# An attention and gated feed-forward kernel on one core: the first eight heads' key and value summaries handled by matrix products instead of copies, and a new order of the opening

## The chip, the core and the metric

The kernel runs on one core of a Trainium2 chip. Five engines work side by side, each through its own list of instructions in order: PE (TensorE, matrix products), DVE (VectorE), ACT (ScalarE), POOL (GpSimd) and SP (which here issues the loads). A wait in one engine's list holds everything behind it in that list. The metric is the time of one execution on the device, in microseconds (us).

## What is computed

`q`, `k`, `v` have 4 batches, 8 heads, 768 positions and 64 features. Attention looks at a band of neighbours and at one summary for each block of 32 keys:

```
k_sum = max of k over each block of 32 ; v_sum = mean of v over each block of 32
scores_l = scale * q @ k.T, kept where |pos_q - pos_k| < 16, else -1e9
scores_s = scale * q @ k_sum.T + log(32)
a = softmax(concat(scores_l, scores_s)) ; x = a @ concat(v, v_sum)
```

The heads are laid side by side (512 features), then a gated layer follows: `h = max(x @ w_in, 0)` (1024 wide), a convolution of three taps over positions, `gate = sigmoid(conv)`, and `(h * gate) @ w_out`. All is in fp32; a product with weights is made of three products of rounded parts (high by high, high by low, low by high).

## The kernel before

**Tiles and stages.** A batch's 768 positions are two chunks of 384. A chunk has four pairs of heads; pair `n` counts through all chunks (`n = 4 * chunk + pair`, so chunk 0 is `n = 0..3`, chunk 1 is `n = 4..7`). For a pair the kernel loads queries, keys and values, makes the key summaries `ks` (a maximum on DVE) and the value summaries `vs` (a sum on DVE, turned by a product `pv` on PE and scaled to means `vm` on ACT), multiplies queries with 96 near keys and 24 summaries for each block of 64 queries (`qk`, 120 columns), masks (`masked`, DVE), exponentiates (`expo`, ACT), normalises (`norm`, POOL or DVE), turns the weights (`turn` on PE, `turned` copies them out) and multiplies with the values (`av`). The result is split in a high and a low part (`xh`, `xl`), goes through `f1` (eight groups `fc` of 128 hidden features, four parts `cc` of three products each), the gates (`R` relu, `T` middle tap, `D` the two other taps on DVE, `H` tanh on ACT, `G` product on DVE, `C` and `O` high and low part) and `f2` (tokens `p` in the opening).

**Two regimes.** Chunks 0 and 1, all decoding of the weights, the attention of chunk 2 and some of chunk 3's are an opening whose order is written out by hand: the string `ORDER` is a list of tokens, each of which is one step with its pair or group number and, after a slash, the engine that does it (`n2.1/v`: normalise head 1 of pair 2 on DVE). Every engine's own list follows the tokens. `Z` tokens are products on zeros that only keep PE busy (`zeros`, L112). From chunk 2 on a loop (`unit`, `slot`, `slot_av`) sets the order; it starts with the turn of pair 12's second head and `f1` of chunk 2. A scheduler orders the loop's instructions on DVE, POOL and SP, and may place them ahead of the last tokens; on PE it follows the code.

**The weights** come as 64-bit words. A weight tile `i` of 16 (8 of `w_in`, 8 of `w_out`) is loaded (`w` or `W`, 512 KB), its words decoded on ACT (`wy`) and DVE (`wl`, `wu`) and split into a high part (`wh`, ACT or POOL) and a low part (`wo`, POOL). The tiles of `w_out` go through the tag `stage`, two buffers, which the value tiles `vt` of later chunks share.

**Chunk 0.** Each pair's keys are loaded once whole (`load_k`), and `key_rows` (tokens `kc`, L146) copies the overlapping near keys from there into `kw`, beside which `key_sums` (tokens `kb`, L271, POOL) repeats the summaries for all six blocks. The value means are repeated in `va` by `val_wide` (tokens `vc`, L295, POOL). Later chunks load near keys and near values ready cut (`load_kw`, `load_v`) and repeat the means by a DMA (`load_vm`).

Of the kernel before, what the change touches and what calls it, by code (L numbers as in the profile page):

```python
# [51 lines left out]
c3.0/s xl2 tr3.1 a6 wy1 wl1 f0.0.0 c3.1/s wu1 av3 wh1/s k10 wl2 wy2 f0.0.1 wo1 xh3/v xl3 w6
f0.0.2 wy3 wu2 f0.1.0 M4 wl3 f0.0.3 wh2/s wu3 f0.1.1 wo2 R0.0/v wh3/s w7 f0.1.2 T0.0/s wy4
wl4 f0.2.0 wo3 D0.0 f0.1.3 a7 wy5 f0.2.1 wu4 R0.1/s q4 H0.0 f0.2.2 wl5 T0.1/s G0.0 wh4/s
f0.2.3 wu5 M5 f0.3.0 C0.0/g D0.1 wh5/s M6 wo4 R0.2/s f0.3.1 T0.2/v H0.1 f0.3.2 q5 wo5 G0.1
D0.2 f0.4.0 C0.1/g f0.3.3 q6 wy6 wl6 f0.4.1 q7 H0.2 wu6 R0.3/s f0.4.2 G0.2 wh6/s f0.5.0 K5
wl7 C0.2/s wo6 wy7 f0.4.3 K6 wy8 f0.5.1 M7 R0.4/s qk4 wu7 wy9 O0.0 f0.5.2 wh7/s q8 K7 wl8
T0.3/s f0.5.3 m4.0 O0.2 W10 e4.0 wu8 m4.1 O0.1 R0.5/s e4.1 wl9 kb5 D0.3 t8 wh8/g T0.4/s
T0.5/s kb6 ks9 wo8 H0.3 ks10 k11 wo7 Z11 p0.0 r4 D0.5 qk5 kb7 n4.1/g q9 D0.4 wy10 K8 n4.0/g
H0.5 G0.3 vs8 tr4.0 H0.4 m5.0 f0.6.0 c4.0/s m5.1 tr4.1 e5.0 f0.6.1 c4.1/s wu9 pv8 e5.1  # L60
f0.6.2 C0.3/g G0.5 wl10 vm8 f0.6.3 kb8 ks11 wh9/s t9 O0.3 av4 t10 C0.5/s r5 R0.6/s wu10 qk6
a8 T0.6/s G0.4 O0.5 xh4/s q10 wh10/s m6.0 f0.7.0 K9 n5.0/g m6.1 e6.0 f0.7.1 xl4 wo10 tr5.0
hx4 e6.1 f0.7.2 vs9 n5.1/g f1.0.0 c5.0/s vs10 t11 f0.7.3 wo9 M8 r6 tr5.1 W11 pv9 D0.6 R0.7/s
# [22 lines left out]
def attention_ffn(ctx, tc, qT, kT, vT, v4, w_in, cwT, w_out, mask8, ident_in, out):  # L86
# [119 lines left out]
    def kw_tile(n):  # L206
        if n == NP - 1:
            kw = sp.tile([P, 1024], F32, tag="stage", name=f"kw{n}", bufs=2)
            of(n)["kw"] = kw[:, : CB * NK].rearrange("p (b k) -> p b k", b=CB)
        else:  # L210
            of(n)["kw"] = sp.tile([P, CB, NK], F32, tag="kw", name=f"kw{n}", bufs=3)
# [608 lines left out]
```

## Time and profile before

| | us |
|---|---|
| median of three runs (lowest, highest) | 401.23 (400.06, 401.51) |
| the profiled execution | 400.0 |
| its span, first to last instruction | 398.2 |

| engine | busy us | share of the span |
|---|---|---|
| PE | 369.2 | 93% |
| DVE | 263.5 | 66% |
| ACT | 236.0 | 59% |
| POOL | 151.6 | 38% |

The span has two parts: up to some 124 us several engines and the loads share the work of the opening, and from there to 394.6 us PE has products without a gap. A mean over both says little; the rows below are taken from each part by itself. A row's "idle before" is the time in which an engine waited ahead of such instructions, and the arrow names what ended the wait.

### The profile page before, as it was taken

The numbers are of one execution on the slowest core, as the hardware profiler recorded it, in microseconds if no ns is written. First come the engines' busy times: TensorE is split into PE (matmuls) and PEld (weight loads), VectorE is DVE, ScalarE is ACT, GpSimd is POOL, SyncE is SP. The second block draws the span as 40 slices with busy tenths as digits, with TensorE's granted clock in tenths as the row PEclk, the third lists the DMA queues.
The fourth block names the chain that finished last, engine by engine and source line by source line (L and its number), as shares of the span: only waits on it lengthen the run. The fifth ranks groups of instructions, "written<-read, shape, count | busy, mean of one in ns | idle before, by whom it ended". The sixth has DMA issues, their size and how long they took to land.

```text
span 398.2 us, 8746 instructions
## 1 busy us (share of the span) xinstructions
PE 369.2 (93%) x3118; PEld 313.2 (79%) x3121; DVE 263.5 (66%) x810; ACT 236.0 (59%) x746; POOL 151.6 (38%) x189
## 2 busy tenths in 40 slices
PE   5768878898996999999999999999999999999996
PEld 2346646687785888888888888988888888999884
DVE  3789899899996465768666556566675755556200
ACT  1765778887564777766565767666656643343211
POOL 2455696776342333333333333333332332222200
PEclk9989999999998999999999999999999999999999
DMA  8999979996755244556332324434310000000011
GB/s 299 316 354 290 239 218 261 286 287 163 251 168 154 81 138 131 159 171 192 77 102 72 97 80 113 114 95 116 93 39 28 28 1 29 26 26 28 26 54 53
DMA packets 45355, 54.29 MB, mean 136 GB/s; under 512 B 24640, under 2 KB 33024, under 8 KB 45312
## 3 DMA queue, kind: packets, MB, share of 16 engines
q1 hardware_dynamic: 41568, 47.19, 41.2%
q10 hardware_dynamic: 3744, 6.54, 4.4%
q8 instruction: 25, 0.41, 0.4%
q14 instruction: 18, 0.15, 0.1%
HBM read 45.36 MB, written 6.29 MB: 130 GB/s over the span
## 4 chain that ended last, share of the span: by engine, by line
PE 70%; DVE 20%; ACT 4%; DMA 3%; issue 2%; SPq 0%; DVEq 0%; ACTq 0%
PE f L615 30%; PE f L512 26%; PE pq L317 5%; PE xp L410 4%; PE pt L394 4%; DVE t L553 4%; DVE a L341 3%; DVE wu L136 2%; ACT a L354 2%; DVE vs L277 2%; DVE wl L130 2%; DVE ks L262 2%; DMA q<-qT 2%; DMA wo<-w_out 1%; DVE a L378 1%
## 5 line engine op out<-in xcount | busy, mean ns | idle before, releaser
L592 POOL TENSOR_TENSOR glo<-t,ghi 128x383 fp32r<-128x383 f32 (+1 forms) x64 | 66.3, 1037 | 125.4 <-ACT ghi L144 110.5
L512 PE MATMUL f<-xh,win_hi 128*128 128x384 f32 (+1 forms) x256 | 91.5, 357 | 4.0 <-DVE t L574 3.5
L553 DVE SCALAR_TENSOR_TENSOR t<-f,cw,t 128x382 f32<-128x382 f32 (+3 forms) x128 | 78.7, 616 | 18.9 <-ACT t L540 15.8
L512 PE MATMUL f<-xh,win_lo 128*128 128x384 f32 (+1 forms) x256 | 87.0, 340 | 1.1 <-POOL win_lo L179 1.1
L512 PE MATMUL f<-xl,win_hi 128*128 128x384 f32 (+1 forms) x256 | 86.7, 339 | 0.0
L354 ACT ACTIVATE a<-a,nm 128x120 f32<-128x120 f32 x192 | 68.7, 399 | 13.3 <-DVE nm L341 12.0
L615 PE MATMUL f<-wout_lo,ghi 128*128 128x512 f32 x192 | 75.4, 393 | 1.0 <-POOL wout_lo L179 1.0
L615 PE MATMUL f<-wout_hi,ghi 128*128 128x512 f32 x192 | 76.0, 396 | 0.3 <-POOL wout_hi L146 0.3
L615 PE MATMUL f<-wout_hi,glo 128*128 128x512 f32 x192 | 74.9, 391 | 0.0
L569 ACT ACTIVATE t<-t 128x383 f32<-128x383 f32 (+1 forms) x64 | 33.7, 527 | 50.0 <-DVE t L553 49.4
L378 POOL TENSOR_TENSOR a<-a,sm 128x360 f32<-128x360 f32 x54 | 42.4, 802 | 48.6 <-DVE sm L373 45.5
L574 DVE SCALAR_TENSOR_TENSOR t<-t,f 128x383 f32<-128x383 f32 (+1 forms) x64 | 35.3, 553 | 31.7 <-ACT t L569 31.7
L512 PEld LDWEIGHTS f<-xh,win_hi 128*128 128x128 f32 x256 | 48.7, 190 | 9.0 <-DVE t L574 5.3
L512 PEld LDWEIGHTS f<-xh,win_lo 128*128 128x128 f32 x256 | 48.4, 189 | 1.7 <-POOL win_lo L179 1.7
L512 PEld LDWEIGHTS f<-xl,win_hi 128*128 128x128 f32 x256 | 48.7, 190 | 1.2
L341 DVE CUSTOM_DVE_ANT_0 a<-pq,mask 128x120 f32<-128x120 f32 x192 | 41.8, 277 | 3.2 <-PE pq L317 2.9
L615 PEld LDWEIGHTS f<-wout_hi,glo 128*128 128x128 f32 x192 | 36.1, 188 | 7.9
L615 PEld LDWEIGHTS f<-wout_hi,ghi 128*128 128x128 f32 x192 | 36.1, 188 | 6.9 <-POOL wout_hi L146 0.8
L394 PE MATMUL pt<-ident,a 128*120 128x128 f32 x192 | 33.4, 283 | 8.6 <-DVE aT L146 3.3
L615 PEld LDWEIGHTS f<-wout_lo,ghi 128*128 128x128 f32 x192 | 36.1, 188 | 6.5 <-POOL wout_lo L179 1.3
L144 ACT COPY aT<-pt 120x384 f32<-120x384 f32 x57 | 28.2, 495 | 18.4 <-PE pt L394 17.8
L530 ACT ACTIVATE f<-f 128x384 f32<-128x384 f32 (+1 forms) x58 | 28.6, 492 | 15.7 <-PE f L512 15.7
(62 smaller groups left out, 465.3 us busy)
## 6 DMA issues: line engine op xcount, KB each, us to landing
va<-v SPq DMA_DIRECT2D x32, 288.0 KB
kw<-kT SPq DMA_DIRECT2D x28, 288.0 KB
q<-qT SPq DMA_DIRECT2D x32, 192.0 KB
out_dram<-ob ACTq DMA_DIRECT2D x24, 256.0 KB
kT<-kT SPq DMA_DIRECT2D x12, 392.0 KB
vt<-vT SPq DMA_DIRECT2D x12, 384.0 KB
wo<-w_out SPq DMA_DIRECT2D x8, 512.0 KB
raw_a<-w_in SPq DMA_DIRECT2D x6, 512.0 KB
```

The lines of the kernel that those rows point to most:

```text
L144: nc.scalar.copy(out, x)
L341: nc.vector.tensor_tensor_reduce(st["a", h][:, i, :], st["pq"][h][:, i * NK : (i + 1) * NK], mask[:, edge(n, i), :], -0.125, 3.0e38, ALU.a ...
L354: this = nc.scalar.activation(st["a", h][:, i, :], st["a", h][:, i, :], AF.Exp, bias=st["nm"][:, h, i : i + 1], scale=-1.0, accum_out=st[" ...
L378: by[eng].tensor_tensor(a, a, s, ALU.mult)
L394: nc.tensor.transpose(pt[:NK, i * P : (i + 1) * P], a[:, i, :], ident)
L512: nc.tensor.matmul(ph[:, :n], w[:, fc, cc, :], x[:, cc, :n], start=(cc == 0 and m == 0), stop=(cc == NCC - 1 and m == 2),)
L530: nc.scalar.activation(h[:, :n], h[:, :n], AF.Relu)
L553: nc.vector.scalar_tensor_tensor(t[:, i0:i1], h[:, hf + k - 1 + i0 : hf + k - 1 + i1], cw[:, fc, k : k + 1], t[:, i0:i1], ALU.mult, ALU.add,)
L569: nc.scalar.activation(t, t, AF.Tanh, scale=0.5)
L574: nc.vector.scalar_tensor_tensor(t, t, 1.0, h[:, hf : hf + ng], ALU.add, ALU.mult)
L592: nc.gpsimd.tensor_tensor(gate_at("lo", c, fc), t, hi.bitcast(F32), ALU.subtract)
L615: nc.tensor.matmul(po, gx[:, fc, ss], w[:, fc, :], start=(fc == 0 and m == 0), stop=(fc == NFC - 1 and m == 2),)
```

## The change

Chunk 0 (pairs 0 to 3) works without the copies. `qk` multiplies with the loaded keys themselves (96 columns), and a new step `q_sums` (token `qs`) multiplies with the summaries (24 columns) for both blocks of 128 queries at once, three blocks and two heads, six products. `val_turn` makes the value sums by six products of the values, loaded with positions on the partitions (`v0`), with a matrix of ones and zeros that stands beside the identity in `consts`; so the four `vs` sums on DVE go. `av` gets one product for each head on the means and twelve on the 96 near values, added up in place. Tokens `kc`, `vc` and four of the `kb` go. `ORDER` is new throughout: the number of tokens of a kind changes only for chunk 0's steps, for the zero products (23 to 43 outside the ten ahead of the list), and for the engine after the slash. From the diff, cut:

```
-k2 k0 t1 k1 q0 k3 q1 ks2 t2 t3 ks0 kc0/g q2 kb0 q3 t0 ks1 kc1/g z qk0 kc2/v kb1 kb2 m0.0 K4
...
-xl10 p1.7 r12 R1.7/s av11 n12.0/v T1.7/s n12.1/g ob1 D1.7 qk13 xh11/s od1 tr12.0 m13.0 H1.7
-xl11 e13.0 G1.7 m13.1 C1.7/g e13.1 c12.0/v O1.7 r13 n13.0/v n13.1/v
+t3 k2 w0 z k0 q0 q1 q2 q3 ks2 pv3 k1 vm3 t2 wy0 wl0 w1 wu0 w2 ks0 K4 Z9 qk0 wh0/v dcw t0 qs0
...
+e11.0 wl14 f1.2.2 D1.1 pv11 tr10.0 e11.1 f1.3.2 wu14 f1.2.3 M12 vm11 c10.0/s r11 f1.3.3 M11
+wh14/s n11.0/v tr10.1 H1.1 n11.1/g R1.2/v qk12 R1.3/s T1.2/s wl15 av9 K15 wo14 G1.1 T1.3/s
...
+e13.0 G1.4 f1.5.3 xl11 e13.1 C1.4/g f1.7.0 R1.5/v p0.1 O1.4 T1.5/v f1.7.1 r13 p0.2 D1.5
+n13.1/g f1.7.2 p0.3 n13.0/v H1.5 f1.7.3 G1.5 C1.5/v p0.4 R1.7/v O1.5 p0.5 p0.6 p0.7 ob0
+f1.6.1 od0 f1.6.2 f1.6.3 R1.6/s T1.6/s T1.7/s D1.6 D1.7 H1.6 G1.6 H1.7 C1.6/v G1.7 O1.6
+C1.7/g O1.7
...
     def val_turn(n):
         pv = ps.tile([P, 512], F32, tag=tag, name=f"pv{n}", bufs=bufs)
-        nc.tensor.transpose(pv[:NB, :P], of(n)["vs"], ident)
+        if n < NP:
+            step = NB // NT
+            for j in range(NT):
+                at = P + NB - step * (j + 1)
+                nc.tensor.matmul(
+                    pv[:NK, :P],
+                    consts[:, at : at + NK],
+                    of(n)["vt"][:, j * P : (j + 1) * P],
+                    start=j == 0,
+                    stop=j == NT - 1,
+                )
+        else:
+            nc.tensor.transpose(pv[:NB, :P], of(n)["vs"], ident)
...
+                if n < NP:
+                    keys = st["k"][r, blk * QB : blk * QB + WK]
+                else:
+                    keys = st["kw"][r, blk, :]
...
+    def q_sums(n):
+        st = of(n)
+        for i in range(CB // 2):
+            for h in range(2):
+                r = slice(h * QB, (h + 1) * QB)
+                nc.tensor.matmul(
+                    st["pq"][h][:, i * NK + WK : (i + 1) * NK],
+                    st["q"][r, i * P : (i + 1) * P],
+                    state["ks", 0, n][r, :],
+                    start=True,
+                    stop=True,
+                )
...
     def av(n):
+        near = WK if n < NP else NK
+        if n < NP:
+            for h in range(2):
+                r = slice(h * QB, (h + 1) * QB)
+                nc.tensor.matmul(
+                    xp[r, :CH],
+                    state["vm", 0, n][:, r],
+                    st["aT", h][WK:NK, :],
+                    start=True,
+                    stop=False,
+                )
```

Tokens that name another engine, counted over the list: `n` on DVE 10 to 5 (on POOL 18 to 23), `c` on DVE 7 to 4, `R` on DVE 6 to 4, `C` on DVE 3 to 2, `T` on DVE 1 to 2, `wh` on DVE 0 to 1 (on POOL 4 to 6, on ACT 12 to 9), `C` on POOL 8 to 6.

The order moves at three places of which the prediction speaks. The first is SP's list from its first load; `k`, `q` and `raw_b` are chunk 0's keys, queries and values, `raw_a` a weight tile, `cw_words` the taps. Before:

```order
L220 DMA k_xl_87<-kT 128x784
L220 DMA k_xh_86<-kT 128x784
L235 DMA raw_b_72<-vT 128x768
L220 DMA k_xh_86<-kT 128x784
L242 DMA q0_97<-qT 128x384
L220 DMA k_xl_87<-kT 128x784
L242 DMA q1_100<-qT 128x384
L235 DMA raw_b_72<-vT 128x768 x2
L242 DMA q2_110<-qT 128x384
L242 DMA q3_113<-qT 128x384
L235 DMA raw_b_72<-vT 128x768
```

and with the change:

```order
L232 DMA raw_b_72<-v0 128x768
L219 DMA k_xl_87<-kT 128x784
L158 DMA raw_a_71<-w_in 128x1024
L678 DMA cw_words_88<-cwT 128x48
L219 DMA k_xh_86<-kT 128x784
L242 DMA q0_98<-qT 128x384
L242 DMA q1_100<-qT 128x384
L242 DMA q2_102<-qT 128x384
L242 DMA q3_104<-qT 128x384
L219 DMA k_xh_86<-kT 128x784
L232 DMA raw_b_72<-v0 128x768
```

A value tile and the first weight tile now stand ahead of pair 0's keys and queries, and three further queries ahead of pair 1's keys.

The second is DVE's list from its first work up to pair 0's first masked scores (`a0_0`). Before:

```order
L262 TENSOR_REDUCE ks2_102<-k_xl_87 128x24
L262 TENSOR_REDUCE ks0_106<-k_xh_86 128x24
L262 TENSOR_REDUCE ks1_116<-k_xh_86 128x24
L146 COPY kw2_135<-k_xl_87 128x6x96
L341 ISA a0_0_141,nm0_139<-pq0_0_121,mask_64 128x120
L341 ISA nm0_139 128x1
```

and with the change:

```order
L262 TENSOR_REDUCE ks2_106<-k_xl_87 128x24
L133 TENSOR_SCALAR wl_0_121<-raw_a_71 128x512
L139 SCALAR_TENSOR_TENSOR wu_0_119<-wu_0_119,wl_0_121 128x512
L262 TENSOR_REDUCE ks0_126<-k_xh_86 128x24
L149 CAST win_hi_67<-wu_0_119 128x512
L133 TENSOR_SCALAR wl_cw_155<-cw_words_88 128x24
L139 SCALAR_TENSOR_TENSOR cw_66<-cw_66,wl_cw_155 128x24
L364 ISA a0_0_168,nm0_166<-pq0_0_139,mask_64 128x120
L364 ISA nm0_166 128x1
```

Three summaries and a copy of keys stood ahead of the scores; now there are two summaries, the decoding of weight tile 0 with its high part, and that of the taps.

The third is DVE's list where the hand-written order ends and the loop begins (`f1_2_0` and `t2_0` are the loop's first group; `ks16` to `ks19`, `vs16`, `vs17` and the edge copies `xh3`, `xl3` are the loop's too, placed there by the scheduler). Before:

```order
L341 ISA nm13_1660 128x1
L146 COPY aT12_0_1680<-pt12_0_1656 120x384
L427 CAST xl3_1790<-xl2_1316 128x4x2
L372 TENSOR_SCALAR sm13_1661<-pq13_0_1640 128x6
L373 RECIPROCAL sm13_1661<-sm13_1661 128x6
L378 TENSOR_TENSOR a13_0_1662<-a13_0_1662,sm13_1661 128x360
L378 TENSOR_TENSOR a13_1_1672<-a13_1_1672,sm13_1661 128x360
L553 SCALAR_TENSOR_TENSOR t2_0_1715<-f1_2_0_1701,cw_66,t2_0_1715 128x382
L553 SCALAR_TENSOR_TENSOR t2_0_1715<-f1_2_0_1701,cw_66,t2_0_1715 128x383
```

and with the change:

```order
L608 SCALAR_TENSOR_TENSOR t1_5_1666<-t1_5_1666,f1_1_5_1565 128x385
L149 CAST ghi_834<-t1_5_1666 128x385
L566 TENSOR_SCALAR f1_1_7_1657<-f1_1_7_1657 128x386
L262 TENSOR_REDUCE ks18_2318<-kT18_2062 128x24
L461 CAST xl3_1838<-xl2_1373 128x4x2
L461 CAST xh3_1837<-xh2_1372 128x4x2
L262 TENSOR_REDUCE ks19_2460<-kT19_2209 128x24
L587 SCALAR_TENSOR_TENSOR t1_6_1719<-f1_1_6_1623,cw_66,t1_6_1719 128x385
L587 SCALAR_TENSOR_TENSOR t1_6_1719<-f1_1_6_1623,cw_66,t1_6_1719 128x384
L587 SCALAR_TENSOR_TENSOR t1_7_1721<-f1_1_7_1657,cw_66,t1_7_1721 128x385
L587 SCALAR_TENSOR_TENSOR t2_0_1763<-f1_2_0_1749,cw_66,t2_0_1763 128x382
L587 SCALAR_TENSOR_TENSOR t1_7_1721<-f1_1_7_1657,cw_66,t1_7_1721 128x384
L608 SCALAR_TENSOR_TENSOR t1_6_1719<-t1_6_1719,f1_1_6_1623 128x385
```

Before, the list ended with pair 13's weights, and the six reduces stood 19 to 95 rows ahead of this piece; now it ends with the gates of chunk 1's groups 6 and 7, behind two of the loop's reduces and its edge copies, one of the loop's own taps is mixed in, and the other four reduces (`ks16`, `vs16`, `ks17`, `vs17`) stand 26, 9, 4 and 1 rows ahead.

## Rows read from the trace of the kernel before

**Rows 1.** Busy time by stretch, the whole core: stretch, its length, then busy us (and number of instructions) of PE, PE's weight loads, DVE, ACT and POOL, the granted clock of PE (1.00 is 2.4 GHz), the share of the DMA engines, and GB/s.
```profile
0.00:11.40 11.40, 7.07 (x37) 2.76 (x37) 4.60 (x16) 2.06 (x6) 3.17 (x10) 1.00 0.86 311
20.00:96.50 76.50, 62.95 (x667) 49.16 (x669) 70.72 (x210) 58.16 (x185) 52.29 (x60) 0.98 0.92 265
96.50:125.10 28.60, 23.68 (x217) 20.07 (x218) 28.29 (x95) 17.87 (x63) 12.20 (x15) 0.96 0.73 217
0.00:125.10 125.10, 99.71 (x984) 75.60 (x988) 110.13 (x348) 84.44 (x282) 71.14 (x90) 0.98 0.88 260
...
124.20:394.60 270.40, 270.36 (x2139) 238.54 (x2137) 154.22 (x464) 151.48 (x465) 80.44 (x99) 1.00 0.27 81
...
120.00:125.00 5.00, 1.72 (x8) 1.70 (x8) 4.93 (x22) 3.22 (x14) 1.77 (x4) 0.77 0.92 264
```

**Rows 2.** The end of the opening on PE, from the timeline: start us, length, engine, line, operation, tiles, and in brackets the wait before it and what ended it.
```profile
123.33 0.87 PE L394 MATMUL pt<-ident,a 128*120 128x128 f32 x3 [3.28 <-DVE aT L146]
123.85 0.67 PE L512 MATMUL f<-xh,win_hi 128*128 128x384 f32 x1
...
126.18 0.34 PE L512 MATMUL f<-xl,win_hi 128*128 128x384 f32 x1
126.35 0.34 PE L512 MATMUL f<-xh,win_lo 128*128 128x384 f32 x1
```

**Rows 3.** DVE's work up to 125 us by line and shape: line, engine, operation, tiles, number | busy us, mean ns of one | idle before.
```profile
L378 DVE TENSOR_TENSOR a<-a,sm 128x360 f32<-128x360 f32 x10 | 6.8, 692 | 0.1
L146 DVE COPY aT<-pt 120x384 f32<-120x384 f32 x7 | 3.9, 551 | 0.0
L277 DVE TENSOR_REDUCE vs<-raw_b 128x24 f32<-128x768 f32 x4 | 3.7, 940 | 0.0
L532 DVE TENSOR_SCALAR f<-f 128x386 f32<-128x386 f32 (+1 forms) x6 | 3.4, 563 | 0.0
L372 DVE TENSOR_SCALAR sm<-pq 128x6 f32<-128x6 f32 x10 | 1.5, 155 | 0.0
L146 DVE CAST ghi<-t 128x385 fp32r<-128x385 f32 x3 | 1.4, 464 | 0.0
L542 DVE TENSOR_SCALAR t<-f,cw 128x383 f32<-128x383 f32 x1 | 0.6, 606 | 0.0
L146 DVE COPY kw<-k_xl 128x576 f32<-128x576 f32 x1 | 0.5, 452 | 0.0
```

**Rows 4.** The chain of waits in order of time, four pieces: start us, us, engine, tile, line. A piece is the step to the next one in the chain, so it is shorter than the instruction where two overlap.
```profile
90.80 0.47 DVE t L574
...
92.40 0.86 DVE ks L262
93.26 0.52 DVE t L553
...
117.86 0.86 DVE ks L262
```

**Rows 5.** The start, from the timeline, columns as in rows 2; the last two are zero products.
```profile
4.88 0.95 DVE L262 TENSOR_REDUCE ks<-k_xl 128x24 f32<-128x768 f32 x1 [3.75 <-DMA k_xl<-kT]
8.78 1.48 PE L317 MATMUL pq<-kw,q 64*64 64x120 f32 x24 [3.15 <-DMA q<-qT]
10.30 0.28 DVE L341 CUSTOM_DVE_ANT_0 a<-pq,mask 128x120 f32<-128x120 f32 x1 [0.82 <-PE pq L317]
...
10.19 1.46 PE L112 MATMUL pw<-idle 128*128 128x512 bf16 x3
...
13.50 0.81 PE L112 MATMUL pw<-idle 128*128 128x512 bf16 x3 [0.28 <-issue]
```

**Rows 6.** PE's small products later on, from the timeline, columns as in rows 2.
```profile
113.08 0.85 PE L317 MATMUL pq<-kw,q 64*64 64x120 f32 x24
113.86 0.54 PE L394 MATMUL pt<-ident,a 128*120 128x128 f32 x3
114.33 0.92 PE L410 MATMUL xp<-aT,va 120*64 120x64 f32 x24
```

**Rows 7.** POOL's work up to 125 us by line and shape, columns as in rows 3.
```profile
L378 POOL TENSOR_TENSOR a<-a,sm 128x360 f32<-128x360 f32 x18 | 14.7, 828 | 7.0 <-DVE sm L373 5.8 <-PE xp L410 0.4 <-ACT aT L144 0.4
L271 POOL COPY kw<-ks 128x144 f32<-128x144 f32 x17 | 5.8, 343 | 5.6 <-PE pq L317 2.9 <-DVE ks L262 2.7
L295 POOL COPY va<-vm 24x768 f32<-24x768 f32 x4 | 3.5, 883 | 4.5 <-ACT vm L291 4.4
L146 POOL COPY kw<-k_xh 128x576 f32<-128x576 f32 x2 | 1.3, 664 | 6.5 <-DMA k_xh<-kT 6.5
```

**Rows 8.** POOL and DVE at 15 us, from the timeline.
```profile
15.02 1.53 POOL L378 TENSOR_TENSOR a<-a,sm 128x360 f32<-128x360 f32 x2 [2.18 <-DVE sm L373]
...
15.98 0.59 DVE L372 TENSOR_SCALAR sm<-sm 128x6 f32<-128x6 f32 x1 [1.12 <-ACT a L354]
```

**Rows 9.** The loads: the traffic of the first 98 us (number of packets, MB, mean rate), then two stretches as in rows 1, then DVE's one long wait for a weight tile, from the timeline.
```profile
DMA packets 18356, 26.69 MB, mean 272 GB/s; under 512 B 9131, under 2 KB 12649, under 8 KB 18344
...
8.00:24.00 16.00, 12.02 (x139) 7.63 (x141) 11.94 (x57) 10.28 (x49) 7.08 (x11) 0.89 1.05 333
40.00:56.00 16.00, 12.74 (x82) 9.42 (x82) 14.79 (x35) 13.03 (x35) 12.32 (x14) 1.00 0.88 226
...
75.73 0.43 DVE L130 TENSOR_SCALAR wl<-wo 128x512 uint32<-128x512 uint32 x1 [1.50 <-DMA wo<-w_out]
```

More of the change, by code (lines that the diff above doesn't have):

```diff
@@ L40 @@
 FIRST = 2
+NT = S // P
+SPAN = NK + NB - NB // NT
 QK_DONE, TR_DONE, AV_DONE = 14, 25, 12
@@ L52 @@
[L52 to L63, printed above, removed]
@@ L82, with attention_ffn @@
+xh11/s n12.1/g G1.3 c12.0/s D1.4 f1.5.1 C1.3/s O1.3 f1.6.0 m13.0 f1.5.2 H1.4 m13.1 p0.0
+e13.0 G1.4 f1.5.3 xl11 e13.1 C1.4/g f1.7.0 R1.5/v p0.1 O1.4 T1.5/v f1.7.1 r13 p0.2 D1.5
+n13.1/g f1.7.2 p0.3 n13.0/v H1.5 f1.7.3 G1.5 C1.5/v p0.4 R1.7/v O1.5 p0.5 p0.6 p0.7 ob0
+f1.6.1 od0 f1.6.2 f1.6.3 R1.6/s T1.6/s T1.7/s D1.6 D1.7 H1.6 G1.6 H1.7 C1.6/v G1.7 O1.6
+C1.7/g O1.7
 """
 @with_exitstack
-def attention_ffn(ctx, tc, qT, kT, vT, v4, w_in, cwT, w_out, mask8, ident_in, out):
+def attention_ffn(ctx, tc, qT, kT, vT, v0, v4, w_in, cwT, w_out, mask8, consts_in, out):
@@ L93, in attention_ffn @@
     mask = cp.tile([P, 3, NK], F32, name="mask")
-    ident = cp.tile([P, P], F32, name="ident")
+    consts = cp.tile([P, P + SPAN], F32, name="consts")
+    ident = consts[:, :P]
     cw = cp.tile([P, NFC, 3], F32, name="cw")
@@ L206, in kw_tile @@
     def kw_tile(n):
[L207 to L211, printed above, removed]
+        of(n)["kw"] = sp.tile([P, CB, NK], F32, tag="kw", name=f"kw{n}", bufs=3)
         return of(n)["kw"]
@@ L263, in key_max @@
         state["ks", n // (2 * NP), n % NP] = ks
-    def key_rows(n, eng):
-        k = of(n)["k"]
-        copy(eng, kw_tile(n)[:, :, :WK], window(k, 1, list(k.ap[0]), WK))
     def key_sums(n):
@@ L289, in val_mean @@
         c, p = divmod(n, NP)
-        vm = cp.tile([NB, P], F32, tag=f"vm{p}", name=f"vm{n}")
-        nc.scalar.activation(vm, of(n)["pv"][:NB, :P], AF.Copy, scale=1.0 / BLK)
+        rows = slice(WK, NK) if n < NP else slice(0, NB)
+        vm = cp.tile([NK, P], F32, tag=f"vm{p}", name=f"vm{n}")[rows, :]
+        nc.scalar.activation(vm, of(n)["pv"][rows, :P], AF.Copy, scale=1.0 / BLK)
         state["vm", c // 2, p] = vm
-    def val_wide(n):
-        nc.gpsimd.tensor_copy(of(n)["va"][WK:NK, :, :], vm_wide(n))
     def first_half(n):
@@ L316, in qk @@
                 r = slice(h * QB, (h + 1) * QB)
+                if n < NP:
+                    keys = st["k"][r, blk * QB : blk * QB + WK]
+                else:
+                    keys = st["kw"][r, blk, :]
                 nc.tensor.matmul(
-                    pq[h][half * QB : (half + 1) * QB, i * NK : (i + 1) * NK],
+                    pq[h][half * QB : (half + 1) * QB, i * NK : i * NK + keys.shape[-1]],
                     st["q"][r, blk * QB : (blk + 1) * QB],
-                    st["kw"][r, blk, :],
+                    keys,
+                    start=True,
[10 more added lines that the diff above has]
+                    state["ks", 0, n][r, :],
                     start=True,
@@ L411, in av @@
                     xp[r, blk * QB : (blk + 1) * QB],
-                    st["va"][:NK, blk, r],
-                    st["aT", h][:NK, blk * QB : (blk + 1) * QB],
-                    start=True,
-                    stop=True,
+                    st["va"][:near, blk, r],
+                    st["aT", h][:near, blk * QB : (blk + 1) * QB],
+                    start=n >= NP,
+                    stop=n >= NP or blk == CB - 1,
                 )
@@ L778 @@
     at = (QB * np.arange(NQ)[:, None] + np.arange(WK)).reshape(-1)
+    blocks = np.zeros((P, SPAN), np.float32)
+    blocks[np.arange(P), NK - NB // NT + np.arange(P) // BLK] = 1.0
     def words(x, shape):
@@ L796 @@
         "vT": heads_t(v),
+        "v0": c(rows[0, :, WIN : WIN + S].reshape(NP, NT, P, P).transpose(0, 2, 1, 3)),
         "v4": c(
```

60 lines of the change are left out of this document (34 added, 26 removed).

## Prediction

> **What bounds the kernel now.** I read the busy times by stretch first, since a mean over the span hides that there are two regimes. From 124.2 to 394.6 us PE is busy for 270.36 of 270.40 us [rows 1], with work that the change does not touch. So whatever the change is worth must be read ahead of that: it is the time at which PE comes out of the opening, the hand-over. The timeline of PE places it: the turn of pair 12's second head starts at 123.33 after a wait of 3.28 us for a copy on DVE, and the loop's first product at 123.85 [rows 2]. That wait costs a little more behind it: the granted clock is 0.77 in that stretch [rows 1], and the seven products from 123.85 to 126.18 take 0.33 us apiece where the next takes 0.17. This is the lower of the two clock levels, and costs some 1.2 us with the turn. I count the old hand-over as 123.3 + 1.2 = 124.5.
>
> Who sets it? In the opening up to 125.1 us DVE is busy for 110.13 us, PE for 99.71, ACT for 84.44, POOL for 71.14 [rows 1]. From 96.5 to 125.1 DVE works 28.29 of 28.60 us, and from 20 to 96.5 it works 70.72 of 76.50 [rows 1]. The chain of waits agrees: ahead of the hand-over it runs from one DVE piece to the next, among them the loop's own reduces at 92.40 and 117.86 [rows 4]. So **DVE bounds the opening**, and 15.0 us of idle time is in it: 8.9 before 20 us (6.8 of it before 11.4), 5.8 up to 96.5 and 0.3 after [rows 1].
>
> **The change, part by part.**
>
> *DVE.* Four sums of values go: 3.7 us [rows 3]. The copy of pair 2's keys goes: 0.45. Five of ten normalisations leave DVE: at the mean of 692 ns [rows 3] 3.5 us, at the 490 ns or so of one that is not held up 2.5; I take 3.0. Three of seven copies of turned weights leave: 3 x 551 ns [rows 3] is 1.65. Two of six relus leave: 2 x 563 ns [rows 3] is 1.1. One of three high parts of gates leaves: 0.46 [rows 3]. A middle tap comes in: 0.6 [rows 3]. A high part of a weight tile comes in, which DVE did not do before: between 0.46 (a cast of 385 columns) and 0.7 (a copy held up by POOL as a normalisation is) [rows 3]; 0.5. Sum: 3.7 + 0.45 + 3.0 + 1.65 + 1.1 + 0.46 - 0.6 - 0.5 = 9.3. Two instructions overlap by up to 0.1 us (a summary of 0.95 us is a step of 0.86 in the chain [rows 4, 5]), so 9.0 are left on the path.
>
> *The start.* The first scores waited for pair 0's queries, 1,752 KB into SP's list, and came at 8.78; DVE's masking began at 10.30 with three summaries and a copy behind it [rows 5]. Now the queries stand 1,896 KB in, and the scores need a summary that follows pair 0's keys; I put the masking at 11.4. By then DVE will have done two summaries, tile 0's two decoding steps and high part, and the taps: 4.3 us of work, against 4.60 by 11.4 us before [rows 1]. No gain, no loss, where the first weight tile is in by some 8 us.
>
> *The end.* Before, DVE was done 1.8 us after PE's hand-over (125.1 against 123.3). Now the gates of groups 6 and 7 stand behind PE's last product: four taps, two gate products and a high part, 4 x 0.52 + 2 x 0.47 + 0.3 = 3.3 us by the chain's steps [rows 4], that PE need not wait for, since their results enter `f2` two loop units later. PE's last twelve us (three parts of group 5, four of 7, eight pieces of `f2`, three of group 6) wait for nothing on DVE, so that the loop's six reduces, which stood in the chain [rows 4], now run beside them. What is late next: the buffer of group 6, which the loop's second group needs some 7 us after the hand-over (12 products of `f1` at 0.17 [rows 2], nine of `f2`, two turns, a `qk` and an `av` [rows 6]); the gate product frees it after about 5.
>
> *The sum.* DVE's end: 125.1 - 9.0 = 116.1. Hand-over: 116.1 - 3.3 = 112.8, if DVE idles as long as before. Against 124.5 that is a gain of 11.7. I take 1.7 off, because the other engines come closer: ACT gains some 1.5 us of work on 84.44 [rows 1] and has 12 us less for it, and the loads and PE come near the same time, as follows. **Gain 10.0: 400.0 becomes 390.0** in terms of the profiled execution. The median of the shown runs lies 1.2 above it, which is within what I can size; the number stays 390.0.
>
> *PE* gets more work. A product in fp32 on the loaded operands leaves two records (24 for the 12 of a `qk`, three for the three turns [rows 6]). The six new value products: as turns 6 x 0.18 = 1.1 us, as two records each 2.2; no row shows one, I take 1.6, less the 0.3 of the turn that goes. The six summary products: 0.4 (half of a `qk`) to 1.0; 0.6. The two on the means: 768 columns, as the twelve in 0.92 us [rows 6], so 0.5 to 0.9; 0.7. A pair: 2.5 us, four pairs 10. The 20 more zero products add 5 to 10, at 0.27 or 0.49 us each [rows 5]. All but the start of it lies where PE was idle for 25.4 of 125.1 us [rows 1], so I cost it at nothing; without that cover it is 15 to 20 us on the path. 99.7 less the loop's 1.2 and with 15 more is 113.5, so PE has just enough room.
>
> *The loads* are the same bytes. The last weight tile now stands 24,720 KB into SP's list (25.6 MB with the ACT queue's), before 23,608 KB. Up to 98 us the queues moved 26.69 MB, 272 GB/s, but 333 where SP had enough to issue [rows 9]. At 280, between the two, the tile lands at 91.4. What stands behind its decoding is, counted from the lists at the chain's steps and PE's rows [rows 4, 6], 21.5 us on DVE and 20.8 on PE up to the hand-over, so 113 to 114: the loads do not bind yet, and leave no slack.
>
> *POOL* loses three key copies (0.66 each), four of the summaries' copies (0.34), four of the means' (0.88) and two high parts, and gains five normalisations (0.83) and two weight parts [rows 7]: a net loss of some 2.5 us. POOL and DVE hold each other up: at 15.98 a small DVE operation takes 0.59 us and ends with POOL's normalisation (15.02 + 1.53) [rows 8], while its like on PSUM takes 0.155 [rows 3]. If each of the five normalisations that POOL gains held DVE for its whole length, 5 x 0.83 = 4.1 us would come back, and the time would be 394.1; if what counts is all of POOL's work, nothing does. I go by the latter, since that work shrinks, and keep 394 as an end of the range.
>
> The Trainium skill, page "SBUF — State Buffer", section "SBUF: two separate sides", has the rule behind this: whichever of a GpSimd operation and a VectorE one in need of the shared port pair starts first holds it for its whole length, and the other stands still. The trace agrees in the row at 15.98; read against this change it gives the 394.1, read over all of POOL the 390.0.
>
> **The rivals.**
> 1. *The loads bind.* For it: SP's list is in order, and a tile of `w_out` waits for one of two buffers that the value sums empty; DVE once waited 1.50 us for such a tile [rows 9]. At 226 GB/s, as from 40 to 56 us [rows 9], for 40 us and 280 else, the last tile lands at 99, the hand-over is 99 + 22.5 = 121.5, and the time 397. Against it: the weights come earlier in the new list, and so does the demand.
> 2. *PE binds, and the kernel is slower.* The new products and zeros come to 10 + 10 us if the clock stays at its lower level (1.2 GHz) for much of the first 45 us; then 98.5 + 20 = 118.5 us are busy, and if half of the 25.4 us idle remains [rows 1], the hand-over is at 131.2 and the time 406.7. It decides from the point where more than 8 us of idle time stay on PE (118.5 + 8 = 126.5, 2 above the old one). For it: a `qk` took 1.48 us at 8.78 and 0.85 at 113 [rows 5, 6]. Against it: the zeros stand in the waits and the products in a stretch where DVE was the bound.
> 3. *DVE waits for the loop.* Its six reduces now stand between the last gates, in order; should each wait for its load (392 KB at 272 GB/s [rows 9] is 1.5 us), 9 of the 10 us go: 399. Against it: their loads are asked for some 10 us ahead.
> 4. *The idle time goes too.* If the new order halves DVE's 8.2 us of idle time after 11.4 us and my 1.7 are not needed, the gain is 11.7 + 4.1 = 15.8: 384.
>
> **How the numbers follow.** Forecast 0.64; loads bind 0.14; PE binds 0.06; DVE waits for the loop 0.06; less idle time 0.10. The forecast's own range is 385.5 to 394.5 (port and idle time). To hold 8 in 10 the range takes in 384 below and the loads' 397 above: 384 to 397. A measurement of this kernel can tell about 0.5%, 2 us, from no change. Faster by more than that: 0.64 + 0.10 + 0.14 = 0.88; within it: 0.06; slower: 0.06.
>
> **What would show it.** The loop's first product near 112 to 115 us, with no wait of 3 us ahead of it and a clock of 1.00; DVE busy for about 101 us up to the end of group 7's gate; PE without a gap over the last twelve us of the opening; the last weight tile decoded near 91; nothing moved after that. I am wrong if the hand-over comes at the foretold time and the loop then waits, if PE's busy time before it exceeds 115 us, if DVE shows waits for loads of over 4 us, or if DVE's busy time does not fall by 8.

## The result and the profile after

| | us |
|---|---|
| changed kernel, median of four runs (lowest, highest) | 390.21 (389.19, 391.24) |
| kernel before, median of four runs beside it | 400.72 (400.06, 401.51) |
| ratio, 95% interval | 0.9737 (0.9699 to 0.9775) |
| the profiled execution of the changed kernel, its span | 391.24, 389.3 |

The median lies 0.2 us from the 390.0 of the forecast, the profiled execution 1.2. The forecast was given in terms of the profiled execution: there the gain is 8.8 us (400.0 to 391.24) where 10.0 were foretold, between the medians 10.5. Medians below are of all runs; the ratios leave out one run of `e1_ops_only` (415.18 us), in which the granted clock was lower than in its others (0.95 against 0.98 to 1.00).

The hand-over first, as in [rows 2]: the timeline of PE in the changed kernel (start us, length, engine, line, operation, tiles, and in brackets the wait before it and what ended it).

```profile
105.11 0.49 PE L417 MATMUL pt<-consts,a 128*120 128x128 f32 x3
107.45 0.44 PE L546 MATMUL f<-xh,win_hi 128*128 128x386 f32 x1 [1.85 <-DVE t L608]
...
115.91 0.34 PE L546 MATMUL f<-xh,win_lo 128*128 128x386 f32 x1
116.08 0.34 PE L546 MATMUL f<-xh,win_hi 128*128 128x384 f32 x1
116.26 0.34 PE L546 MATMUL f<-xl,win_hi 128*128 128x384 f32 x1
```

The products on 384 positions from 116.08 on are the loop's. The first follows the last product of group 6 with no wait, and its successors come every 0.17 us. So the hand-over moved from 124.5 to 116.1, 8.4 us, where 114.5 and 10.0 were foretold. In the last 12 us PE waits once, at 107.45. The hand-over is indeed all that counts: in the profiled executions of the changed kernel (both of them) and of ten of the experiments below, the time is the loop's first product plus 275.0 to 275.2 us. Two have more: the kernel before (276.2, with the slow products of [rows 2]) and `e1_ops_only` (277.7, where the granted clock is 0.75 for 11 us behind its hand-over).

The busy times by stretch, in the columns of [rows 1], for the changed kernel:

```profile
0.00:11.40 11.40, 9.47 (x31) 4.93 (x31) 2.77 (x5) 2.33 (x4) 0.20 (x4) 1.00 0.87 312
...
0.00:122.40 122.40, 115.19 (x1184) 90.00 (x1185) 101.27 (x337) 86.35 (x290) 67.08 (x83) 1.00 0.87 268
...
116.10:385.70 269.60, 269.58 (x2139) 237.83 (x2137) 157.85 (x472) 153.61 (x468) 83.09 (x102) 1.00 0.28 83
...
0.00:45.00 45.00, 41.72 (x424) 28.43 (x425) 28.47 (x114) 23.26 (x88) 18.41 (x25) 1.00 0.95 309
45.00:75.00 30.00, 28.08 (x304) 22.24 (x301) 29.35 (x99) 28.58 (x93) 23.77 (x28) 1.00 0.88 257
75.00:100.00 25.00, 24.85 (x276) 21.38 (x275) 24.00 (x79) 23.45 (x81) 17.17 (x23) 1.00 0.78 221
```

and the last three stretches in the kernel before:

```profile
0.00:45.00 45.00, 31.71 (x286) 21.00 (x288) 34.56 (x99) 25.28 (x81) 21.38 (x30) 0.96 1.00 307
45.00:75.00 30.00, 24.62 (x243) 18.72 (x245) 27.47 (x90) 23.84 (x82) 22.63 (x28) 1.00 0.87 243
75.00:100.00 25.00, 22.68 (x258) 18.79 (x257) 23.31 (x77) 19.97 (x66) 17.36 (x21) 1.00 0.85 242
```

Up to 122.4 us, where group 7's gate product ends, DVE works 101.27 us, as foretold (101). But the first 45 us hold 16.5 us of DVE's idle time, 6.1 more than before. Behind 45 us the picture turns: from 45 to 100 PE, DVE and ACT are each busy for 95 to 97% of the time.

The times at which a few pieces end or start, read from the timelines, for this and some of the experiments below (us):

| | first masking | chunk 0's last `xl` ends | chunk 1's last `xl` ends | weight tile 15 decoded | loop's first product |
|---|---|---|---|---|---|
| before | 10.3 | 35.6 | 85.8 | 98.0 | 123.8 |
| after | 13.5 | 47.5 | 78.7 | 95.8 | 116.1 |
| `e1_ops_only` (new operations, old order) | 11.1 | 41.1 | 91.1 | 103.3 | 129.2 |
| `a3_old_ops` (old operations, new order) | 12.6 | 48.0 | 79.2 | 96.3 | 114.8 |
| `g1_old_engines` (old engines behind 75 us) | 12.1 | 46.0 | 78.7 | 98.9 | 122.4 |

The new order lets chunk 0 come 12 us later and chunk 1's attention 7 us earlier: weights, `f1` and attention are mixed where before they came in blocks.

### The profile page after: what moved, and what is told of

The parts are those of the page before. It is cut to its first block, busy times and chain, and to the rows that moved or that the text cites. A ratio compares the mean times of both kernels' runs of the same rounds, so it can differ in the third digit from the quotient of the medians.

```text
span 389.3 us, 8973 instructions
## 1 busy us (share of the span) xinstructions
PE 378.5 (97%) x3249; PEld 322.4 (83%) x3249; DVE 253.3 (65%) x796; ACT 236.1 (61%) x750; POOL 149.4 (38%) x183
## 4 chain that ended last, share of the span: by engine, by line
PE 80%; DVE 8%; DMA 6%; ACT 2%; issue 1%; POOL 1%; SPq 1%; ACTq 0%; DVEq 0%; POOLq 0%
PE f L649 33%; PE f L546 30%; PE xp L444 5%; PE pt L417 5%; PE pq L327 4%; DMA kT<-kT 3%; DVE a L364 2%; DVE t L587 2%; DMA raw_b<-w_in 2%; PE pv L285 1%; DVE ks L262 1%; DMA consts<-consts 1%; DMA wo<-w_out 1%; DVE wu L139 1%; DVE t L608 1%
## 5 line engine op out<-in xcount | busy, mean ns | idle before, releaser
L626 POOL TENSOR_TENSOR glo<-t,ghi 128x383 fp32r<-128x383 f32 (+1 forms) x64 | 65.3, 1020 | 115.8 <-ACT ghi L147 100.3
L546 PE MATMUL f<-xh,win_hi 128*128 128x386 f32 (+1 forms) x256 | 91.1, 356 | 3.1 <-DVE t L608 2.9
L546 PE MATMUL f<-xl,win_hi 128*128 128x386 f32 (+1 forms) x256 | 86.5, 338 | 0.0
L546 PE MATMUL f<-xh,win_lo 128*128 128x386 f32 (+1 forms) x256 | 86.4, 338 | 0.0
L401 POOL TENSOR_TENSOR a<-a,sm 128x360 f32<-128x360 f32 x59 | 47.8, 825 | 60.4 <-DVE sm L396 55.7
L608 DVE SCALAR_TENSOR_TENSOR t<-t,f 128x383 f32<-128x383 f32 (+1 forms) x64 | 35.4, 553 | 30.9 <-ACT t L603 30.9
L147 ACT COPY aT<-pt 120x384 f32<-120x384 f32 x60 | 29.9, 499 | 16.8 <-PE pt L417 16.6
L564 ACT ACTIVATE f<-f 128x384 f32<-128x384 f32 (+1 forms) x60 | 29.5, 492 | 13.9 <-PE f L546 13.9
L147 ACT CAST ghi<-t 128x383 fp32r<-128x383 f32 (+1 forms) x56 | 28.9, 516 | 12.5 <-DVE t L608 12.1
```

The lines of the kernel that those rows point to most:

```text
L147: nc.scalar.copy(out, x)
L401: by[eng].tensor_tensor(a, a, s, ALU.mult)
L546: nc.tensor.matmul(ph[:, :n], w[:, fc, cc, :], x[:, cc, :n], start=(cc == 0 and m == 0), stop=(cc == NCC - 1 and m == 2),)
L564: nc.scalar.activation(h[:, :n], h[:, :n], AF.Relu)
L608: nc.vector.scalar_tensor_tensor(t, t, 1.0, h[:, hf : hf + ng], ALU.add, ALU.mult)
L626: nc.gpsimd.tensor_tensor(gate_at("lo", c, fc), t, hi.bitcast(F32), ALU.subtract)
```

## The experiments

### Operations and order apart

`e1_ops_only`: the changed program with the old list.

```
-ks0 kc0/g q2 kb0 q3 t0 ks1 kc1/g z qk0 kc2/v kb1 kb2 m0.0 K4
+ks0 q2 q3 t0 ks1 z qk0 qs0 m0.0 K4
...
```

> Chunk 0's new operations in the old order: the tokens of the removed steps are taken out of the old list and each new summary product stands right behind its scores; nothing else moves. Theory A (DVE's work sets the opening): the four sums and the key copy, 4.1 us, leave DVE, and the hand-over comes some 3.5 to 4 us earlier: 396.7 to 397.2, where before is 400.7. Theory B (the order is what holds the opening; the new products fill PE where it has waits): 399 to 402.

Measured: 410.42 us, ratio 1.0243 (1.0187 to 1.0299). Both theories missed, A by its sign: chunk 0's new operations make the old order slower. (The old list was kept with its engines; "order" in this part means the whole list, the sequence of the tokens and the engine behind each slash.) The timeline of PE shows where (the profiled execution took 406.87 us, the least of its six; lines stand one lower; columns as above):

```profile
9.58 1.48 PE L339 MATMUL pq<-ks,q 64*128 64x24 f32 x12
...
12.38 1.39 PE L326 MATMUL pq<-k_xh,q 64*64 64x96 f32 x24
...
23.86 2.88 PE L284 MATMUL pv<-raw_b,consts 128*120 128x128 f32 x24
26.67 0.86 PE L433 MATMUL xp<-aT,vm 24*64 24x384 f32 x4
27.46 0.92 PE L443 MATMUL xp<-aT,va 96*64 96x64 f32 x24
28.31 0.54 PE L416 MATMUL pt<-consts,a 128*120 128x128 f32 x3
28.69 1.47 PE L284 MATMUL pv<-raw_b,consts 128*120 128x128 f32 x12
```

PE has hardly a wait from 8.4 to 42 us, with its products at the slower rate at first (the summary products take 1.48 us at 9.58, 0.85 later); chunk 0's last `xl` ends 5.5 us late, and the loop's first product is 5.4 us late. The other executions took 0.5 to 8.3 us longer than this one, and what they lost more was not seen. The cover on which the prediction put PE's new products, PE's idle time, is not in this order's first 40 us.

`a3_old_ops`: the other way round, the program of before with the new list.

```
-ks2 pv3 k1 vm3 ... Z9 qk0 ... pv0 e2.1 kb4 a2 ... vm0
+ks2 vs3 pv3 k1 vm3 ... Z9 kc0/g kb0 qk0 ... vs0 pv0 e2.1 kb4 a2 vc2 ... vm0 vc0
```

> The kernel before with the new order: chunk 0's old steps are put back into the new list (each key copy and its repeated summaries ahead of its scores, each value sum ahead of its turn, each copy of the means behind the means and the value load; pair 4's key load goes two loads later and pair 3's summary three tokens earlier, as their buffers need). DVE gets 4.1 us back, POOL some 6, PE loses some 12. Theory A (the order carries the gain, the operations little): 390 to 394. Theory B (the new order only works with chunk 0's new operations, as the sums and copies stand in the chain of the first 45 us): 395 to 401. By DVE's removed work alone (the prediction's sum): 390.2 + 4.1 = 394.3.

Measured: 389.24 us, ratio 0.9727 (0.9695 to 0.976); theory A, to beyond its end. Its stretches, in the columns of [rows 1]:

```profile
0.00:45.00 45.00, 34.87 (x316) 21.13 (x317) 33.43 (x119) 22.09 (x84) 23.27 (x36) 0.89 0.96 303
45.00:75.00 30.00, 27.39 (x302) 21.85 (x301) 29.42 (x98) 28.65 (x96) 23.92 (x27) 1.00 0.88 259
75.00:100.00 25.00, 24.92 (x278) 21.73 (x277) 24.00 (x78) 23.39 (x82) 17.39 (x22) 1.00 0.78 225
```

DVE works 5.0 us more and PE 6.9 less in the first 45 us than in the changed kernel, chunk 0 ends within 0.6 us of it, and from 45 to 100 us the rows are the same to 0.1 us on DVE and ACT. So **the new list carries the whole gain; in it, chunk 0's new operations as a set give nothing.** The four sums and the key copy, 4.1 us of the prediction's 9.0, came back as idle time: DVE idles 11.6 us of the first 45 with them and 16.5 without. Whether DVE would have waited there anyway, or now waits for the new products on PE, this pair of runs does not tell (see `d2_pv1`).

### Which engine does the work, and where

`g1_old_engines`: the new order, but 27 tokens from pair 7's copies on with their old engines.

```
-c7.0/s ... n10.0/g ... n10.1/g ... R1.3/s ... C1.1/g ... T1.4/v ... c12.0/s ...
+c7.0/v ... n10.0/v ... n10.1/v ... R1.3/v ... C1.1/v ... T1.4/s ... c12.0/v ...
```

> The changed kernel with the engines of before for the tokens of the last third of the opening's order (27 tokens from pair 7's copies to pair 13's weights; the order stays, and the gates of groups 6 and 7 keep their engines). DVE gets back six copies of turned weights for one that leaves, six normalisations for one, two relus and two high parts, and gives up two middle taps: 3.3 - 0.55 + 3.45 + 1.1 + 0.8 - 1.2 = 6.9 us of work, all of it behind 75 us. Theory A (DVE sets the pace from 45 us on, and the change's gain is the work it was relieved of there): the hand-over comes 5 to 7 us later, 395 to 397. Theory B (the order of the tokens and the end carry the gain, whoever does the work): 390 to 392.

Measured: 397.47 us, ratio 0.9942 (0.992 to 0.9963); the changed kernel itself beside it, `r_after`:

> The changed kernel itself once more, beside the next three, so that differences of 1 us among them can be read: 389 to 391 by every theory.

389.66 us, 0.9737 (0.9719 to 0.9756). So 7.8 us, theory A, somewhat above its range. The waits of PE up to 125 us in `g1_old_engines` (what waited and for what: us in total, times, longest):

```profile
PE f L545 <- DVE t L607: 7.8, 7, 2.6
```

and in the changed kernel, up to 122 us (3.6 in all in `r_after`):

```profile
PE f L546 <- DVE t L608: 2.9, 4, 1.9
```

`f1` waits for a PSUM buffer that DVE's gate product (L608, here L607) frees. For the 6.9 us that DVE got, the loop's first product comes 6.5 us later (122.4 against 115.9 in `r_after`). Not all of it need be DVE's work: right behind the longest of these waits, which ends at 109.6, the granted clock reads 0.60 (columns of [rows 1]), and by that share some 1.6 us are slower products (an estimate, 0.4 of 4 us).

```profile
110.00:114.00 4.00, 4.00 (x16) 3.67 (x15) 3.83 (x19) 0.53 (x1) 1.00 (x1) 0.60 1.05 341
```

So most of the change's gain hangs on which engine does these 27 steps. That is shown for the new order; the new engines in the old order were not run, and the 7.8 us here and the 3.8 of `e3_old_end` below come to more than the whole gain, so they are not separate shares of it.

`d1_no_wl`: the same from the other side, 3.6 us taken from DVE.

```
-        join(state["wu", i], state["wl", i])
+        join(state["wu", i], state["wl", min(i, NFC - 1)])
 (and the tokens wl8 to wl15 leave the list)
```

> The changed kernel without DVE's first decoding step (0.45 us) for the eight tiles of the second weight matrix: the second step joins the low bits of tile 7 to all of them, so their low bits are left out. DVE loses 3.6 us of work between 43 and 95 us, where it was busy for 53.4 of 55 us. Theory A (DVE bounds this stretch, as predicted for the whole opening): 386.6 to 387.5. Theory B (PE at 52.9 and ACT at 52.0 of the 55 us are as full, so that an engine by itself can give next to nothing): 389 to 390.4.

Measured: 386.62 us, ratio 0.9659 (0.9627 to 0.9691), so 3.0 us below the changed kernel, theory A. PE and ACT, as full as DVE by their busy time, did not hold it back. Chunk 1's last `xl` ends at 76.5 us (77.4 in `r_after`), the loop's first product starts at 111.6 (115.9): most of it comes behind 77 us.

`f2_both_pool` takes two normalisations from DVE instead, on top of the two edits of the next part:

```
-n8.0/v ... n11.0/v
+n8.0/g ... n11.0/g
```

> The same two edits, and DVE's two normalisations of pairs 8 and 11 (0.55 to 0.7 us each, between 70 and 100 us) on POOL, which was busy for 40.9 of 55 us there. Theory A (DVE sets the pace there): another 0.8 to 1.2 us, 386.6 to 387.6. Theory B (POOL's normalisation of 0.83 us holds DVE up or comes late for its turn on PE): 387.8 to 389.5.

Measured: 389.24 us, ratio 0.9735 (0.9713 to 0.9756), nothing beside `f1_both` (0.9726), and within theory B's range. DVE's timeline shows what took the place of the work, in this kernel and then in `f1_both`:

```profile
91.65 1.44 DVE L132 TENSOR_SCALAR wl<-wo 128x512 uint32<-128x512 uint32 x1 [1.31 <-DMA wo<-w_out]
```
```profile
91.03 1.23 DVE L132 TENSOR_SCALAR wl<-wo 128x512 uint32<-128x512 uint32 x1 [0.47 <-DMA wo<-w_out]
```

DVE is ready for the last weight tile at 90.3 instead of 90.6, but the tile is there 0.6 us later; in `r_after` the wait is 0.27 us, ending at 91.87. When the tile comes is set by DVE itself: SP asks for it as soon as a value sum on DVE empties its buffer (in `r_after` the sum ends at 87.06 and the load is asked for at 87.10), and it lands 4.8 us later. The two normalisations that left DVE do not bring that sum forward.

### The end of the opening

`e3_old_end`: the kernel before with one token moved, the copy that PE waited for at 123.33 [rows 2].

```
-tr12.0 m13.0 H1.7 xl11 e13.0 G1.7 m13.1 C1.7/g e13.1 c12.0/v O1.7
+tr12.0 c12.0/v m13.0 H1.7 xl11 e13.0 G1.7 m13.1 C1.7/g e13.1 O1.7
```

> The kernel before with one token moved: DVE's copy of pair 12's first turned weights, for which PE waited 3.28 us at 123.33, stands ahead of pair 13's masking instead of behind it, behind the turn itself. Theory A (the end of the order is worth something by itself): DVE reaches the copy 1.3 us of masking, 0.5 of a low part and 0.5 of a gate product earlier, so that PE waits 1 to 1.5 us instead of 3.3, and the lower clock behind it may go (1.2 us): 397.5 to 399. Theory B (DVE is merely late, and the next thing the loop needs from it is late by the same): 400.2 to 400.9.

Measured: 395.77 us where before is 399.72, ratio 0.9905 (0.9868 to 0.9943): 3.8 us, theory A, beyond its range (1.7 to 3.2 us were foretold). The profiled execution shows what is left of the wait:

```profile
120.31 0.52 PE L393 MATMUL pt<-ident,a 128*120 128x128 f32 x3 [1.13 <-DVE aT L145]
```

2.1 us less, and the clock behind it is the upper level (1.00 from 96.5 to 125, against 0.96 before), so that the slow products of [rows 2] go too, 1.2 us. That makes 3.3; this execution was also 0.7 us ahead at chunk 0's last `xl`, where the token had not acted yet (34.9 against 35.6), which is spread. Over a third of the gain of the large change can be had from one token, by that alone.

`b1_k16`: the one wait that is left at the new end. The chain of waits of the changed kernel gives its cause (start us, us, engine, tile, line):

```profile
96.50 0.87 PE xp L444 x24
97.38 0.02 issue
97.39 0.34 SPq L249
97.73 0.04 issue
97.77 6.44 DMA kT<-kT
104.21 0.02 issue
104.24 0.95 DVE ks L262
...
106.93 0.48 DVE t L608
107.41 0.04 issue
107.45 0.79 PE f L546 x3
```

Pair 16's keys, which the loop's first hoisted reduce needs, stand in SP's list behind pair 14's values, whose buffer the `av` at 96.50 frees.

```
-wo14 G1.1 T1.3/s m12.0 wy15 f1.4.0 a13
+wo14 G1.1 T1.3/s m12.0 wy15 f1.4.0 k16 a13
```

> The changed kernel with one load moved in SP's list: the keys of pair 16, which the loop asks for behind a value load that waits for a buffer until 97.4 us, are asked for two value loads earlier. The summary on DVE at 104.24 waited 1.7 us for them, and behind it stood the gate product for which PE waited 1.85 us at 107.45. Theory A (the loop's reduce delays the opening, the prediction's third rival in small): both waits go, 388.3 to 389. Theory B (the work behind is late anyway): 389.8 to 390.6.

Measured: 388.87 us, ratio 0.9743 (0.9701 to 0.9785). In the profile both waits shrink as theory A has it, PE's to 0.56 us, and the loop's first product starts at 113.8 (115.9 in `r_after`); the median lies in theory A's range too. But the ratio is that of the changed kernel, whose own executions spread over 2.3 us, so whether the load is worth a microsecond is not shown.

### The start and PE's products

`c1_start`:

```
-ks2 pv3 k1 vm3 t2 wy0 wl0 w1 wu0 w2 ks0 K4 Z9 qk0
+ks2 pv3 k1 wy0 vm3 t2 wl0 w1 wu0 w2 ks0 K4 Z4 qk0
```

> The changed kernel with a shorter start: on ACT the first decoding step of weight tile 0 stands ahead of pair 3's means (which wait for the constants' load), not behind it, and the zero products ahead of the first scores are 4, not 9. DVE's masking, which began at 13.5 us, can begin at 11.4 to 12. Theory A (chunk 0's chain from the first scores on is on the path up to the hand-over): 388.2 to 389.2. Theory B (the first weight tiles and loads set the pace behind it, so the time is given back): 389.8 to 390.6.

Measured: 389.44 us, ratio 0.973 (0.9697 to 0.9763), between the two theories; masking starts at 12.2, as it does in `r_after` without the edit. `f1_both` has this and `b1_k16`'s load:

> The changed kernel with the earlier load of pair 16's keys and the shorter start together. Theory A (both act on one chain, one after the other): the 1.4 us of the start and the 1 us of the load add up, 387.6 to 388.4. Theory B (the spread of the start from run to run is all that there was): 389 to 390.2.

Measured: 389.17 us, ratio 0.9726 (0.9706 to 0.9745); masking starts at 11.1, the loop's first product at 114.2. The median is in theory B's range, 0.5 us below `r_after` (389.66), and the intervals do not tell the two apart. Between the profiled executions nothing is given back on the way: `f1_both` is ahead of `r_after` by 1.1 us at the first masking, 1.0 at chunk 1's last `xl` and at the decoding of tile 15 (95.0 against 96.0), 1.7 at the loop's first product. So a gain of about a microsecond is neither shown nor ruled out.

`e4_no_zeros`: all `Z` tokens leave the list.

```
-... ks0 K4 Z9 qk0 ... k3 ks1 Z7 qk1
+... ks0 K4 qk0 ... k3 ks1 qk1
```

> The changed kernel without the 43 zero products of the order's list (the ten ahead of the list stay). Theory A (DVE bounds, as predicted: zeros cost nothing): 389.5 to 391 as long as the clock holds. Theory B (PE bounds the stretch from 20 to 41 us, where DVE waits 6.7 us for four results of PE and 17 zero products of 0.22 us stand): DVE's waits shrink by up to 3.7 us, and the time is 386.5 to 389. Theory C (the zeros hold the granted clock up): the clock falls to its lower level in parts of the first 45 us, and the time is 391 to 396.

Measured: 391.33 us, ratio 0.9786 (0.9742 to 0.983), at the lower end of theory C's range. The clock is 0.84 from 20 to 45 us and 0.93 from 45 to 96.5, where the changed kernel has 1.00; PE's busy time from 20 to 45 falls by 1.8 us only, since the other products take longer. So the zeros cost nothing and do hold the clock up; in time they may be worth a microsecond, but the interval overlaps that of the changed kernel.

`d2_pv1`: one of six value products for each pair.

```
-            for j in range(NT):
+            for j in range(1):
```

> The changed kernel with one of the six value products of each of chunk 0's pairs: five sixths of the values are left out of the block means. PE loses 20 products of some 0.26 us, 5.2 us, 4 of them between 16 and 30 us. Theory A (PE is on the path of the first 41 us, where DVE waits 6.7 us for it): chunk 0's last low part ends 2 to 4 us earlier than at 47.5, and the time is 386.5 to 388.5. Theory B (DVE bounds, as predicted; these products cost nothing): 389.5 to 390.6.

Measured: 386.55 us, ratio 0.9652 (0.9618 to 0.9686), 3 us below the changed kernel, as theory A has it. But its profiled execution took 389.28 us and the four others 385.67 to 387.22, and in the profiled one chunk 0's last `xl` ends at 45.9 us, hardly before the 46.2 of `r_after`. So the value products have a price of some 3 us between the medians, 1.6 between the profiled executions, and the place where it is paid was not seen.

## Why the prediction was right, point by point

**DVE's sum: right in size, wrong in place.** DVE's work up to group 7's gate fell from 110.1 to 101.3, 8.8 us for 9.0. The step that failed is the next one, "DVE's end: 125.1 - 9.0 = 116.1 ... if DVE idles as long as before". Group 7's gate product ended at 122.4, with 21.1 us of idle time where 15.0 + 1.7 were assumed. The 4.1 us of sums and key copy came back as waits in the first 45 us (`a3_old_ops`), by themselves or through PE's products that replace them. What paid was the relief behind 75 us, 6.9 us of tokens on other engines (`g1_old_engines`), which the prediction had as part of a net 5.1 over the whole opening: in the first 45 us the new order puts work on DVE that other engines did (three copies or casts, two normalisations, a weight tile's high part, less two normalisations; about 2 us by [rows 3]), into its waits. A sum over the opening could not tell the two.

**The end: right in kind, and larger.** The gates of groups 6 and 7 stand behind PE's last product, the loop does not wait at the hand-over, and the clock is at its upper level. Group 7's gate product ended 6.3 us behind the hand-over, not 3.3, because one of the loop's reduces, its edge copies, two of its taps and a wait of 0.4 us are mixed in; PE did not need it. That the end matters is shown by `e3_old_end`, where one token at the old end was worth 3.8 us. So the errors offset each other: group 7's gate came 4.6 us later than the 114.5 + 3.3 foretold, and 3.0 of that did not matter, which leaves the 1.6 by which the hand-over missed. That the median then fell within 0.2 us of 390.0 is in part luck: 4.1 us of the sum gave nothing, and the end covered most of the lack.

**The first rival's loads: "no slack", as said.** The last tile was put at 91.4 us; where DVE was ready before it, the wait for it ended at 91.0 to 92.2 (`f1_both`, `c1_start`); in the first profile of the changed kernel DVE came to it at 92.9 without a wait. It took back what `f2_both_pool` won on DVE.

**The third rival in small.** One of the loop's six reduces waited for its load, 1.7 us on DVE and 1.85 on PE; the rival's place was right, its 9 us were not; what the removal of the wait is worth stays open (`b1_k16`).

**PE.** The prices, from the changed kernel's timeline (columns as above):

```profile
16.47 1.57 PE L285 MATMUL pv<-raw_b,consts 128*120 128x128 f32 x12
18.30 0.73 PE L327 MATMUL pq<-k_xl,q 64*64 64x96 f32 x24
18.96 0.85 PE L340 MATMUL pq<-ks,q 64*128 64x24 f32 x12
...
25.08 0.86 PE L434 MATMUL xp<-aT,vm 24*64 24x384 f32 x4
25.87 0.92 PE L444 MATMUL xp<-aT,va 96*64 96x64 f32 x24
```

Value products 1.57 (1.6 was taken), summaries 0.85 (0.6), means 0.86 (0.7), less 0.3 for the turn that went and 0.12 on the scores: 2.9 us a pair, not 2.5. The sum for PE came out too high all the same: it was busy for 108.9 us up to the hand-over, not 113.5. "Cost nothing" is not right: PE's idle time fell from 25.4 to 7.2 us up to the hand-over. In the old order the operations cost 5 us and more (`e1_ops_only`), and in the new one the value products some 3 (`d2_pv1`); with the sums and copies that they replace the account is even (`a3_old_ops`). The second rival, "PE binds", did not come with the new order but for these 3 us; in the old order it is what the operations do.

**The start.** Masking began at 13.5 instead of 11.4 (12.2 in the second profile), held by the constants' load, pair 3's products at the slower rate, and ACT's list:

```profile
6.38 2.89 PE L285 MATMUL pv<-raw_b,consts 128*120 128x128 f32 x12 [0.74 <-DMA consts<-consts]
```
```profile
9.30 0.27 ACT L300 ACTIVATE vm<-pv 24x128 f32<-24x128 f32 x1 [6.36 <-PE pv L285]
9.60 0.66 ACT L122 ACTIVATE wu<-raw_a 128x512 f32<-128x512 f32 x1
```
```profile
10.29 0.69 DVE L139 SCALAR_TENSOR_TENSOR wu<-wu,wl 128x512 uint32<-128x512 uint32 x1 [2.57 <-ACT wu L122]
```

It cost nothing that can be measured (`c1_start`).

**POOL.** Five more normalisations on POOL could hold DVE up by 4.1 us, which made 394.1. Of that nothing shows in like instructions: DVE's groups up to 116 us, columns as in [rows 3], where these took 692 and 551 ns:

```profile
L401 DVE TENSOR_TENSOR a<-a,sm 128x360 f32<-128x360 f32 x5 | 3.4, 688 | 0.1
L149 DVE COPY aT<-pt 120x384 f32<-120x384 f32 x4 | 2.2, 549 | 2.3 <-PE xp L444 2.3
```

Single instructions are still held up, as in [rows 8]: the decoding step at 91.65 above takes 1.44 us, where its like takes 0.43 [rows 9], and ends 0.3 us behind POOL's low part, which began just before it:

```profile
91.52 1.28 POOL L181 TENSOR_TENSOR wout_lo<-wu,wout_hi 128x512 fp32r<-128x512 f32 x1
```

The Trainium skill, page "SBUF — State Buffer", section "SBUF: two separate sides", has it that whichever of a GpSimd and a VectorE operation in need of the shared port pair starts first holds it for its whole length; the trace agrees in this row. For the sum it was right to go by all of POOL's work, which fell from 71.1 to 66.3 us up to the hand-over; no run here varies that work alone.

## What to carry to other kernels

Work taken off the busiest engine paid here only in the stretch where that engine sets the pace: split its busy and idle time by stretch before summing, and ask of each removed instruction whether the engine waits right behind it. When operations and order change together, run the two crosses (new operations in the old order, and the reverse); here they are +2.4% and -2.7%, and the sum by operations alone would have named the wrong cause. Look at the last wait before a hand-over first: one token there was worth 1% here. And read a difference of one microsecond only where it is larger than the spread of one kernel's own executions (2.3 us in `r_after`).
